# One explicit order for all TensorE instructions of a fused retention and adapter kernel

## The chip, the cores and the metric

The kernel runs on one core of a Trainium2 chip. The metric is the device time of one execution in microseconds, as the median of several runs. TensorE (PE) does the matrix work, VectorE (DVE), ScalarE (ACT) and GpSimd (POOL) the elementwise work, and SyncE (SP) issues nearly all transfers.

## The reference

Two steps follow each other. The first is a causal attention without softmax, in which the score of a query and a key is scaled by 1/8 and by a decay `gamma[h] ** (i - j)`; the second sends each token through two of eight adapters of rank 16.

```python
q, k, v: (8, 8, 576, 64) float32        # batch, heads, sequence, head dimension
scores = scale * q @ k.T
ret    = scores * where(i >= j, gamma[h] ** (i - j), 0)
x      = (ret @ v) as (4608, 512)       # 4608 tokens, 8 heads x 64
logits = x @ w_gate                     # (4608, 8)
w      = softmax over the two largest logits
out    = x + sum over those two e of  w_e * ((x @ A[e]) @ B[e])
```

All of `x @ A[e]` and `x @ w_gate` is made in one product with 128 + 8 columns; `z` is masked with the weights and goes through all of `B` in one product.

## The kernel before

The sequence of 576 is cut into four chunks of 128 rows and a last one of 64. A quad is four batch entries of one chunk: it is what one group of loads brings (twelve transfers of 256 KB, four each for q, k and v). A unit is two batch entries of one quad, all eight heads. There are 18 units: four per chunk for the four full chunks (units 0 to 15) and two for the short one (units 16 and 17). The sums over earlier chunks are carried in `P`, one per unit position, so unit t reads what unit t - 4 left.

For each unit t the program runs these stages, each a burst of TensorE instructions and the work of another engine on its result:

- T (L173, pqT and pkT, L186): 16 transposes of q and 16 of k, 64 rows by 128 columns each. `b` alternates fastest, so that neighbouring transposes take the lower and the upper 64 rows of the array. ACT copies the results to qT and kT (L195).
- Q (L201, px, L213): products of 64 by 64 with the carried sums, 32 instructions in the trace (a float32 product is two there, a transpose one); left out in the first chunk.
- S (L222, pe and pl, L238): the scores, 64 instructions in the trace; DVE multiplies them with the causal mask (re L250, rl L263).
- R (L269, px, L285): masked scores times v, on top of Q; DVE scales the result to xT (L297).
- U (L307, pu, L318): the new carried sum, 64 instructions; DVE adds the old one (pn L333) and POOL applies the decay (P L334).
- Z (L368, pz, L373): 16 instructions of the full 128 by 128 array; DVE then makes lg (L386), two maxima, ns (L389), cm (L399) and zc (L405), with a sigmoid on ACT between ns and cm.
- B, X and Y (L338, L356, L413) finish the unit: B transposes xT into po (16 instructions, L345), X transposes zc (pzt, L360), Y adds the product with `Bcat` to po (L421); ACT copies po to osb (L431), and SP stores it.

The main loop (L454 to L471) writes them in the order Q(t), S(t), T(t+1), B(t-1), R(t), U(t), X(t-1), Z(t), Y(t-1). POOL scales v for the next unit (L166). The loads of a quad are written two quads ahead, into three sets of buffers.

The order in the program text is not the order on the engines. A compile-time scheduler places the instructions of each engine by what it estimates to be ready, and the pools hand out buffers as it goes. Two pools lie in PSUM: `pxp` with two buffers for px, and `pp` with six buffers of one tag, which all other products share. A product that takes over a buffer waits until the engine that reads the earlier one is through. On the chip each engine then works through its own list in order.

Three shapes of array are used: 64 by 128 (the transposes T and B), 64 by 64 (Q, S, R, U) and 128 by 128 (X, Z, Y). In the order of the kernel before, the shape changes 165 times over 3036 products and transposes, and 318 transposes follow one that used the same 64 rows.

Of the kernel before, what the change touches and what calls it, by code (L numbers as in the profile page):

```python
# [18 lines left out]
def kernel(  # L19
# [10 lines left out]
    nc = tc.nc  # L30
# [34 lines left out]
    dr_first = nc.inline_tensor(id64_np, "c_first")  # L65
    dr_asc = nc.inline_tensor(asc_np.astype(np.float32), "c_asc")
    dr_rest = nc.inline_tensor(rest_np, "c_rest")

    cpool = ctx.enter_context(tc.tile_pool(name="consts", bufs=1))
    iop = ctx.enter_context(tc.tile_pool(name="io", bufs=3))  # L70
# [102 lines left out]
    def stage_T(t):  # L173
        c, qd, sl = units[t]
        full = c < NFULL
        qt, kt, vt = nat[(c, qd)]
        s = {}
        for nm in ("qT", "kT"):
            dst = wk.tile([128, 2, HP, C], FP32, tag=nm, name=nm)
            ps = [pp.tile([128, HP, 2, L], FP32, tag="pb", name=f"p{nm}") for _ in range(2)]  # L180
            for hp in range(HP):
                for x, (e, sx) in enumerate(parts(t)):
                    for b in range(2):
                        h2 = slice(2 * hp, 2 * hp + 2)
                        lhs = (kt if nm == "kT" else qt)[e][rows(b), sx, h2, :]
                        nc.tensor.matmul(  # L186
                            ps[b][:, hp, x, :],
                            lhsT=lhs,
                            rhs=id64[rows(b), :],
                            is_transpose=True,  # L190
                            start=True,
                            stop=True,
                        )
            for b in range(2):
                nc.scalar.copy(  # L195
                    out=dst[:, b].rearrange("p a (x i) -> p a x i", x=2), in_=ps[b]
                )
            s[nm] = dst
        st[t] = s

    def stage_Q(t):  # L201
        c, qd, sl = units[t]
        s = st[t]
        s["px"] = px = [pxp.tile([128, HP, C], FP32, tag="px", name="px") for _ in range(2)]
        if c == 0:
            return
        n = 1 if c < NFULL else 2
        w = C // n
        for hp in range(HP):
            for x in range(n):  # L210
                for ho in range(2):
                    for b in range(2):
                        nc.tensor.matmul(  # L213
                            px[b][rows(ho ^ b), hp, w * x : w * x + w],
                            lhsT=P[(qd, sl + x)][b][rows(ho), hp, :],
                            rhs=s["qT"][rows(ho), b, hp, w * x : w * x + w],
                            start=(hp == 0 and x == 0),
                            stop=False,
                            skip_group_check=True,
                        )  # L220

    def stage_S(t):  # L222
        c, qd, sl = units[t]
        full = c < NFULL
        s = st[t]
        pe = [pp.tile([128, HP, C], FP32, tag="pb", name=f"pe{ho}") for ho in range(2)]
        pl = [pp.tile([128, HP, L], FP32, tag="pb", name=f"pl{ho}") for ho in range(2)] if full else []
        for x in range(2):
            for hp in range(HP):
                for b in range(2):  # L230
                    for ho in range(2):
                        if x == 1 and full:
                            o = pl[ho][rows(b), hp, :]
                        else:
                            o = pe[ho][rows(b), hp, (L * x if not full else 0) : (C if full else L * x + L)]
                        i0 = L * x
                        i1 = C if full else L * x + L
                        nc.tensor.matmul(  # L238
                            o,
                            lhsT=s["kT"][rows(ho), b, hp, L * x : L * x + L],  # L240
                            rhs=s["qT"][rows(ho), b, hp, i0:i1],
                            start=(hp == 0 and (x == 0 or full)),
                            stop=True,
                            skip_group_check=True,
                        )
        s["re"], s["rl"] = [], []
        for ho in range(2):
            r = wk.tile([128, HP, C], FP32, tag=f"re{ho}", name=f"re{ho}")
            if full:
                nc.vector.tensor_tensor(  # L250
                    out=r, in0=pe[ho],
                    in1=triE.unsqueeze(1).broadcast_to((128, HP, C)), op=ALU.mult,
                )
            else:
                nc.vector.tensor_tensor(
                    out=r.rearrange("p a (x i) -> p (a x) i", x=2),
                    in0=pe[ho].rearrange("p a (x i) -> p (a x) i", x=2),
                    in1=tri.unsqueeze(1).broadcast_to((128, HP * 2, L)), op=ALU.mult,
                )
            s["re"].append(r)  # L260
        for ho in range(len(pl)):
            r = wk.tile([128, HP, L], FP32, tag=f"rl{ho}", name=f"rl{ho}")
            nc.vector.tensor_tensor(  # L263
                out=r, in0=pl[ho],
                in1=tri.unsqueeze(1).broadcast_to((128, HP, L)), op=ALU.mult,
            )
            s["rl"].append(r)

    def stage_R(t):  # L269
        c, qd, sl = units[t]  # L270
        full = c < NFULL
        s = st[t]
        px = s["px"]
        vt = nat[(c, qd)][2]
        for x, (e, sx) in enumerate(parts(t)):
            for hp in range(HP):
                for ho in range(2):
                    for b in range(2):
                        if full and x == 1:
                            w = s["rl"][ho][rows(b), hp, :]  # L280
                        elif full:
                            w = s["re"][ho][rows(b), hp, :]
                        else:
                            w = s["re"][ho][rows(b), hp, L * x : L * x + L]
                        nc.tensor.matmul(  # L285
                            px[b][rows(ho ^ b), hp, L * x : C if full else L * x + L],
                            lhsT=vt[e][rows(b), sx, 2 * hp + ho, :],
                            rhs=w,
                            start=(c == 0 and hp == 0 and x == 0),
                            stop=True,  # L290
                            skip_group_check=True,
                        )
        s["xT"] = []
        for b in range(2):
            xt = mo.tile([128, HP, C], FP32, tag="xT", name="xT", bufs=6)
            if full:
                nc.vector.tensor_tensor(out=xt, in0=px[b], in1=asc[b], op=ALU.mult)  # L297
            else:
                nc.vector.tensor_tensor(
                    out=xt.rearrange("p a (x i) -> p a x i", x=2),  # L300
                    in0=px[b].rearrange("p a (x i) -> p a x i", x=2),
                    in1=asc[b][:, :, 0:L].unsqueeze(2).broadcast_to((128, HP, 2, L)),
                    op=ALU.mult,
                )
            s["xT"].append(xt)

    def stage_U(t):  # L307
# [5 lines left out]
        for hp in range(HP):  # L313
            for e in range(2):
                for ho in range(2):
                    for b in range(2):
                        h = 2 * hp + ho
                        nc.tensor.matmul(  # L318
                            pu[b][rows(ho), hp, :],
                            lhsT=kt[e][rows(b), sl, h, :],  # L320
                            rhs=vt[e][rows(b), sl, h, :],
                            start=(hp == 0 and e == 0),
                            stop=(e == 1),
                            skip_group_check=True,
                        )
# [12 lines left out]
    def stage_B(t):  # L338
# [3 lines left out]
        for g in range(2):  # L342
            for dt in range(HP):
                for cc in range(2):
                    nc.tensor.matmul(  # L345
                        po[cc][:, g, dt, :],
                        lhsT=s["xT"][g][rows(cc), dt, :],
                        rhs=id64[rows(cc), :],
# [7 lines left out]
    def stage_X(t):  # L356
        s = st[t]
        pzt = pp.tile([128, 2, 128], FP16, tag="pb", name="pzt")
        for g in range(2):
            nc.tensor.matmul(  # L360
                pzt[:, g, :], lhsT=s["zc"][:, g, :], rhs=ident16,
                is_transpose=True, start=True, stop=True,
            )
# [4 lines left out]
    def stage_Z(t):  # L368
        s = st[t]
        pz = pp.tile([128, 2, ER + E], FP32, tag="pb", name="pz")  # L370
        for g in range(2):
            for dt in range(HP):
                nc.tensor.matmul(  # L373
                    pz[:, g, :],
                    lhsT=s["xT"][g][:, dt, :],
                    rhs=AW[g][:, dt, :],
# [36 lines left out]
    def stage_Y(t):  # L413
# [4 lines left out]
        bv = Bcat.rearrange("p (a o d) -> p a o d", a=HP, o=2)  # L418
        for cc in range(2):
            for g in range(2):  # L420
                nc.tensor.matmul(  # L421
                    po[cc][:, g, :, :],
                    lhsT=s["zT"][:, g, :],
                    rhs=bv[:, :, cc ^ g, :],
# [80 lines left out]
```

## Time and profile before

| | us |
|---|---|
| runs shown | 254.44, 257.71, 264.52 (median 257.71) |
| profiled execution | 254.11 |
| its span, first to last instruction | 251.9 |
| PE busy | 211.1 (84%) |
| DVE, ACT, POOL busy | 104.7, 76.7, 57.5 |
| mean granted clock | 0.968 |

A unit ends on TensorE with Z, and DVE starts lg within 0.1 us of that, so the starts of lg mark the units. A matmul of the trace is a pair with its weight load; matmuls overlap, so the length of a burst is read from the start of one burst to the start of the next. "x16" in a row is the number of instructions that were merged into it. The profile carries the line numbers of the kernel before.

### The profile page before, as it was taken

How to read it: one execution, taken by the hardware profiler on the slowest of the kernel's cores; microseconds unless marked ns; L12 is line 12 of the kernel's file. 1: busy time of each engine (PE TensorE's matmuls, PEld its weight loads, DVE VectorE, ACT ScalarE, POOL GpSimd, SP SyncE). 2: the span in 40 equal slices, each digit the busy share in tenths (PEclk: the TensorE clock that was granted, in tenths of full speed). 3: DMA queues.
4: the chain of work that ended last, by engine and by line, in shares of the span. 5: the costliest groups of instructions: out<-in, count | busy, mean ns of one | idle time of the engine just before them, and what ended most of it. 6: DMA issues, size and time to landing. Idle time of an engine off the chain costs nothing.

```text
span 251.9 us, 11229 instructions
## 1 busy us (share of the span) xinstructions
PE 211.1 (84%) x5100; PEld 183.3 (73%) x5100; DVE 104.7 (42%) x282; ACT 76.7 (30%) x200; POOL 57.5 (23%) x72
## 2 busy tenths in 40 slices
PE   1787989799998997989789879989798979997970
PEld 0576878687878785978678768878597868987850
DVE  0032262563235436551835254623555173474440
ACT  2302123521361123411243135313341124532431
POOL 1250204105002052203520080206220342071000
PEclk9996599999999999999999999999999999999995
DMA  5887798998998980689339940879178004831233
GB/s 114 215 130 163 175 226 201 222 229 207 203 274 193 222 222 4 173 197 204 103 108 202 225 145 18 218 175 233 37 191 227 9 0 138 196 113 69 85 87 83
DMA packets 123071, 39.29 MB, mean 156 GB/s; under 512 B 118032, under 2 KB 118288, under 8 KB 123024
## 3 DMA queue, kind: packets, MB, share of 16 engines
q1 hardware_dynamic: 122880, 38.44, 62.9%
q8 instruction: 40, 0.66, 1.1%
q0 software_dynamic: 144, 0.13, 0.3%
q14 instruction: 7, 0.06, 0.1%
HBM read 29.26 MB, written 9.44 MB: 154 GB/s over the span
## 4 chain that ended last, share of the span: by engine, by line
PE 63%; DVE 17%; SPq 7%; ACT 6%; issue 3%; DMA 1%; ACTq 0%; DVEq 0%
PE pz L373 15%; PE px L285 12%; PE px L213 8%; PE pu L318 7%; PE pkT L186 5%; PE pqT L186 5%; DVE cm L399 5%; SPq L126 5%; PE po L345 4%; DVE re L250 4%; PE pe L238 3%; ACT qT L195 3%; DVE ns L389 2%; DVE xT L297 2%; PE po L421 2%
## 5 line engine op out<-in xcount | busy, mean ns | idle before, releaser
L334 POOL TENSOR_TENSOR P<-pn,gdec 128x256 f32<-128x256 f32 x24 | 17.0, 729 | 126.1 <-DVE pn L333 126.1
L166 POOL TENSOR_TENSOR v<-v,pack 128x512 f32<-128x512 f32 x36 | 36.6, 1044 | 34.0 <-DMA v<-in_v_dram 34.0
L195 ACT COPY qT<-pqT 128x512 f32<-128x512 f32 x36 | 20.1, 588 | 69.3 <-PE pqT L186 69.3
L373 PE MATMUL pz<-AW,xT 128*128 128x136 f32 x288 | 40.0, 294 | 1.2 <-DVE pn L333 0.9
L297 DVE TENSOR_TENSOR xT<-px,asc 128x512 f32<-128x512 f32 x32 | 20.6, 686 | 43.8 <-PE px L285 43.8
L373 PEld LDWEIGHTS pz<-AW,xT 128*128 128x128 f32 x288 | 36.4, 198 | 2.2 <-ACT zT L365 1.1
L195 ACT COPY kT<-pkT 128x512 f32<-128x512 f32 x36 | 20.4, 595 | 55.6 <-PE pkT L186 55.5
L186 PE MATMUL pqT<-id,q 64*128 64x64 f32 x288 | 24.4, 238 | 7.6 <-DMA q<-in_q_dram 6.9
L285 PE MATMUL px<-re,v 64*64 64x128 f32 (+1 forms) x640 | 25.8, 272 | 4.1 <-issue 1.5
L186 PE MATMUL pkT<-id,k 64*128 64x64 f32 x288 | 27.0, 242 | 1.6 <-DMA k<-in_k_dram 1.1
L431 ACT COPY osb<-po 128x256 f32<-128x256 f32 x72 | 22.4, 395 | 16.4 <-PE po L421 16.4
L186 PEld LDWEIGHTS pqT<-id,q 64*128 64x128 f32 x288 | 18.8, 143 | 11.7 <-issue 6.8
L213 PE MATMUL px<-qT,P 64*64 64x128 f32 (+1 forms) x512 | 21.0, 264 | 5.0 <-DVE xT L297 4.2
L186 PEld LDWEIGHTS pkT<-id,k 64*128 64x128 f32 x288 | 20.0, 146 | 6.9 <-issue 2.5
L285 PEld LDWEIGHTS px<-re,v 64*64 64x64 f32 x640 | 18.5, 136 | 7.8 <-DVE re L250 3.2
L250 DVE TENSOR_TENSOR re<-pe,triE 128x512 f32<-128x512 f32 x32 | 20.5, 681 | 8.2 <-PE pe L238 8.1
L318 PE MATMUL pu<-v,k 64*64 64x64 f32 x1024 | 23.6, 227 | 0.2 <-ACT qT L195 0.2
L238 PE MATMUL pe<-qT,kT 64*64 64x128 f32 (+1 forms) x640 | 22.8, 271 | 0.9 <-ACT kT L195 0.9
L213 PEld LDWEIGHTS px<-qT,P 64*64 64x64 f32 x512 | 16.8, 133 | 7.7 <-ACT qT L195 4.0
L318 PEld LDWEIGHTS pu<-v,k 64*64 64x64 f32 x1024 | 20.3, 139 | 1.5 <-ACT qT L195 0.3
L238 PEld LDWEIGHTS pe<-qT,kT 64*64 64x64 f32 x640 | 18.7, 138 | 3.4 <-issue 1.7
L238 PE MATMUL pl<-qT,kT 64*64 64x64 f32 x512 | 14.2, 227 | 7.3 <-DVE zc L405 7.3
(35 smaller groups left out, 177.7 us busy)
## 6 DMA issues: line engine op xcount, KB each, us to landing
q<-in_q_dram SPq DMA_DIRECT2D x32, 256.0 KB, 5.1
k<-in_k_dram SPq DMA_DIRECT2D x32, 256.0 KB, 5.1
v<-in_v_dram SPq DMA_DIRECT2D x32, 256.0 KB, 5.1
out_dram<-osb SPq DMA_DIRECT2D x32, 256.0 KB, 3.3
q<-in_q_dram SPq DMA_DIRECT2D x8, 128.0 KB, 3.8
k<-in_k_dram SPq DMA_DIRECT2D x8, 128.0 KB, 3.4
v<-in_v_dram SPq DMA_DIRECT2D x8, 128.0 KB, 3.2
out_dram<-osb SPq DMA_DIRECT2D x8, 128.0 KB, 2.4
```

Source lines behind the costliest of these rows:

```text
L166: nc.gpsimd.tensor_tensor(out=vv, in0=vv, in1=gv[:, e].unsqueeze(2).broadcast_to((128, H, Dh)), op=ALU.mult,)
L186: nc.tensor.matmul(ps[b][:, hp, x, :], lhsT=lhs, rhs=id64[rows(b), :], is_transpose=True, start=True, stop=True,)
L195: nc.scalar.copy(out=dst[:, b].rearrange("p a (x i) -> p a x i", x=2), in_=ps[b])
L213: nc.tensor.matmul(px[b][rows(ho ^ b), hp, w * x : w * x + w], lhsT=P[(qd, sl + x)][b][rows(ho), hp, :], rhs=s["qT"][rows(ho), b, hp, w * ...
L238: nc.tensor.matmul(o, lhsT=s["kT"][rows(ho), b, hp, L * x : L * x + L], rhs=s["qT"][rows(ho), b, hp, i0:i1], start=(hp == 0 and (x == 0 or ...
L250: nc.vector.tensor_tensor(out=r, in0=pe[ho], in1=triE.unsqueeze(1).broadcast_to((128, HP, C)), op=ALU.mult,)
L285: nc.tensor.matmul(px[b][rows(ho ^ b), hp, L * x : C if full else L * x + L], lhsT=vt[e][rows(b), sx, 2 * hp + ho, :], rhs=w, start=(c == ...
L297: nc.vector.tensor_tensor(out=xt, in0=px[b], in1=asc[b], op=ALU.mult)
L318: nc.tensor.matmul(pu[b][rows(ho), hp, :], lhsT=kt[e][rows(b), sl, h, :], rhs=vt[e][rows(b), sl, h, :], start=(hp == 0 and e == 0), stop=( ...
L334: nc.gpsimd.tensor_tensor(out=pn, in0=tmp, in1=gdec, op=ALU.mult)
L373: nc.tensor.matmul(pz[:, g, :], lhsT=s["xT"][g][:, dt, :], rhs=AW[g][:, dt, :], start=(dt == 0), stop=(dt == HP - 1), skip_group_check=True,)
L431: nc.scalar.copy(out=osb[:, g, :, cc ^ g, :], in_=po[cc][:, g])
```

## The change

Every matmul and every transpose now goes through a helper `mm`, which gives it a dependency, without a semaphore, on the TensorE instruction that was written before it. So the scheduler must keep TensorE's instructions in the order of the program text. All nine calls of `nc.tensor.matmul` become `mm` with the same arguments; two of them are shown.

```diff
@@ -66,6 +66,17 @@
     dr_asc = nc.inline_tensor(asc_np.astype(np.float32), "c_asc")
     dr_rest = nc.inline_tensor(rest_np, "c_rest")
 
+    order = mybir.DependencyInfo(mybir.DependencyClass.NoSync, mybir.DependencyReason.DATA)
+    queued = {}
+
+    def mm(*args, **kw):
+
+        i = nc.tensor.matmul(*args, **kw)
+        i = getattr(i, "ins", i)
+        if "pe" in queued:
+            tc.add_manual_dep(i, queued["pe"].name, order, reason="program order")
+        queued["pe"] = i
+
...
@@ -183,7 +194,7 @@
                         lhs = (kt if nm == "kT" else qt)[e][rows(b), sx, h2, :]
-                        nc.tensor.matmul(
+                        mm(
                             ps[b][:, hp, x, :],
...
@@ -282,7 +293,7 @@
-                        nc.tensor.matmul(
+                        mm(
                             px[b][rows(ho ^ b), hp, L * x : C if full else L * x + L],
```

The counts over the new order are 74 changes of shape, and no transpose after one of the same 64 rows. The lists of DVE and SP keep their order; those of ACT and POOL change in places.

The first place is TensorE in unit 11, between S(11) and Z(11). Rows carry the line of the call, the operation, output and inputs with their buffer numbers, and the output's partitions by elements; pqT_2927 and pqT_2928 are the two halves of T(12), px_2864 and px_2865 belong to R(11). Before:

```order
L238 MATMUL pl1_2885<-qT_2683,kT_2704 64x64
L186 MATMUL pqT_2927<-id64_73,q320_2097 128x64
L186 MATMUL pqT_2928<-id64_73,q320_2097 128x64
L285 MATMUL px_2864<-re0_2918,v320_1597 64x128
L186 MATMUL pqT_2927<-id64_73,q321_2098 128x64
L186 MATMUL pqT_2927<-id64_73,q320_2097 128x64
L186 MATMUL pqT_2927<-id64_73,q321_2098 128x64
L186 MATMUL pqT_2927<-id64_73,q320_2097 128x64
L186 MATMUL pqT_2927<-id64_73,q321_2098 128x64
L186 MATMUL pqT_2927<-id64_73,q320_2097 128x64
L186 MATMUL pqT_2927<-id64_73,q321_2098 128x64
L285 MATMUL px_2865<-re0_2918,v320_1597 64x128
```

The same place now (L74 is the line inside the helper):

```order
L74 MATMUL pl1_2885<-qT_2683,kT_2704 64x64
L74 MATMUL pqT_2927<-id64_73,q320_2097 128x64
L74 MATMUL pqT_2928<-id64_73,q320_2097 128x64
L74 MATMUL pqT_2927<-id64_73,q321_2098 128x64
L74 MATMUL pqT_2928<-id64_73,q321_2098 128x64
L74 MATMUL pqT_2927<-id64_73,q320_2097 128x64
L74 MATMUL pqT_2928<-id64_73,q320_2097 128x64
L74 MATMUL pqT_2927<-id64_73,q321_2098 128x64
L74 MATMUL pqT_2928<-id64_73,q321_2098 128x64
```

R(11) stood between the transposes and split them by halves; now the 32 transposes of T(12) and the 16 of B(10) stand together ahead of R(11), and the halves alternate.

The second place is TensorE around the end of Z(11): pz_3069 is Z(11), pkT_2949 one half of T(12), po0_2968 and po1_2969 are Y(10), px_3116 and px_3117 are Q(12), pe0_3134 is S(12). Before:

```order
L373 MATMUL pz_3069<-AW1_82,xT_3020 128x136 x4
L186 MATMUL pkT_2949<-id64_73,k321_2100 128x64
L186 MATMUL pkT_2949<-id64_73,k320_2099 128x64
L186 MATMUL pkT_2949<-id64_73,k321_2100 128x64
L186 MATMUL pkT_2949<-id64_73,k320_2099 128x64
L186 MATMUL pkT_2949<-id64_73,k321_2100 128x64
L186 MATMUL pkT_2949<-id64_73,k320_2099 128x64
L186 MATMUL pkT_2949<-id64_73,k321_2100 128x64
L421 LDWEIGHTS zT_3067
L421 MATMUL po0_2968<-Bcat_83,zT_3067 128x256
```

Now:

```order
L74 MATMUL pz_3069<-AW1_82,xT_3020 128x136 x4
L74 LDWEIGHTS zT_3067
L74 MATMUL po0_2968<-Bcat_83,zT_3067 128x256
L74 LDWEIGHTS zT_3067
L74 MATMUL po0_2968<-Bcat_83,zT_3067 128x256
L74 LDWEIGHTS zT_3067
L74 MATMUL po1_2969<-Bcat_83,zT_3067 128x256
L74 LDWEIGHTS zT_3067
L74 MATMUL po1_2969<-Bcat_83,zT_3067 128x256
L74 MATMUL px_3116<-qT_2926,P000_2309 64x128
L74 MATMUL px_3117<-qT_2926,P001_2313 64x128
```

The late half of the k transposes is gone from here, and Q(12), which stood before U(11), has moved behind Y(10).

The third place is POOL in units 8 and 9: P_2309 and P_2313 belong to unit 8, P_2552 and P_2556 to unit 9, and v_1597 and v_1598 are the v of the quad of units 10 and 11. Before:

```order
L334 TENSOR_TENSOR P_2309<-pn_2310,gdec 128x256
L334 TENSOR_TENSOR P_2313<-pn_2314,gdec 128x256
L334 TENSOR_TENSOR P_2552<-pn_2553,gdec 128x256
L334 TENSOR_TENSOR P_2556<-pn_2557,gdec 128x256
L166 TENSOR_TENSOR v_1597<-v_1597,pack 128x512 x2
L166 TENSOR_TENSOR v_1598<-v_1598,pack 128x512 x2
```

Now:

```order
L345 TENSOR_TENSOR P_2309<-pn_2310,gdec 128x256
L345 TENSOR_TENSOR P_2313<-pn_2314,gdec 128x256
L177 TENSOR_TENSOR v_1597<-v_1597,pack 128x512 x2
L345 TENSOR_TENSOR P_2552<-pn_2553,gdec 128x256
L345 TENSOR_TENSOR P_2556<-pn_2557,gdec 128x256
L177 TENSOR_TENSOR v_1598<-v_1598,pack 128x512 x2
```

The four scalings of v that followed every second unit are now two after each unit.

## Rows read from the trace of the kernel before

**Rows 1.** The page: span, busy time by engine, the main DMA queue.

```profile
span 251.9 us, 11229 instructions
...
PE 211.1 (84%) x5100; PEld 183.3 (73%) x5100; DVE 104.7 (42%) x282; ACT 76.7 (30%) x200; POOL 57.5 (23%) x72
...
q1 hardware_dynamic: 122880, 38.44, 62.9%
```

**Rows 2.** Windows: stretch, length, busy PE PEld DVE ACT POOL, clock, DMA share, GB/s.

```profile
24.00:31.00 7.00, 7.00 (x54) 6.15 (x58) 0.87 (x3) 1.17 (x2) 2.08 (x2) 0.50 0.76 171
67.40:223.50 156.10, 138.39 (x3505) 121.19 (x3506) 72.86 (x192) 50.26 (x133) 37.01 (x45) 1.00 0.62 156
```

**Rows 3.** DVE timeline, lg after Z(1), Z(3), Z(15), Z(17): start, length, instruction.

```profile
42.15 0.17 DVE L386 COPY lg<-pz 128x16 f32<-128x16 f32 x1 [1.88 <-PE pz L373]
...
67.41 0.17 DVE L386 COPY lg<-pz 128x16 f32<-128x16 f32 x1 [1.88 <-PE pz L373]
...
223.56 0.17 DVE L386 COPY lg<-pz 128x16 f32<-128x16 f32 x1 [1.24 <-PE pz L373]
...
242.79 0.17 DVE L386 COPY lg<-pz 128x16 f32<-128x16 f32 x1 [1.61 <-PE pz L373]
```

**Rows 4.** PE timeline in units 10 and 11; in brackets idle time and releaser.

```profile
151.46 0.69 PE L238 MATMUL pl<-qT,kT 64*64 64x64 f32 x30 [1.46 <-DVE zc L405]
...
155.19 1.10 PE L285 MATMUL px<-re,v 64*64 64x128 f32 x32
...
157.63 0.28 PE L360 MATMUL pzt<-ident,zc 128*128 128x128 f16 x2
157.77 2.09 PE L373 MATMUL pz<-AW,xT 128*128 128x136 f32 x16
...
165.31 0.64 PE L186 MATMUL pqT<-id,q 64*128 64x64 f32 x7
...
167.11 1.47 PE L213 MATMUL px<-qT,P 64*64 64x128 f32 x26 [0.89 <-DVE xT L297]
...
169.09 0.76 PE L345 MATMUL po<-id,xT 64*128 64x64 f32 x16
169.78 1.14 PE L318 MATMUL pu<-v,k 64*64 64x64 f32 x58
```

**Rows 5.** PE timeline of unit 15, S and the q transposes in one piece.

```profile
215.64 0.64 PE L238 MATMUL pl<-qT,kT 64*64 64x64 f32 x32
216.21 0.71 PE L186 MATMUL pqT<-id,q 64*128 64x64 f32 x16
216.76 0.65 PE L186 MATMUL pkT<-id,k 64*128 64x64 f32 x8
```

**Rows 6.** DVE timeline after Z(9) and after Z(10).

```profile
147.70 0.17 DVE L386 COPY lg<-pz 128x16 f32<-128x16 f32 x1 [1.88 <-PE pz L373]
...
149.37 1.64 DVE L399 SCALAR_TENSOR_TENSOR cm<-lg,m,sg 128x8 f32<-128x8 f32 x2 [0.37 <-ACT sg L394]
150.93 0.48 DVE L405 TENSOR_TENSOR zc<-pz,cm 128x128 f16<-128x128 f32 x2
...
159.90 0.17 DVE L386 COPY lg<-pz 128x16 f32<-128x16 f32 x1 [1.01 <-PE pz L373]
...
161.37 0.48 DVE L405 TENSOR_TENSOR zc<-pz,cm 128x128 f16<-128x128 f32 x2
162.26 1.29 DVE L250 TENSOR_TENSOR re<-pe,triE 128x512 f32<-128x512 f32 x2 [0.41 <-PE pe L238]
163.46 0.74 DVE L263 TENSOR_TENSOR rl<-pl,pack 128x256 f32<-128x256 f32 x2
```

**Rows 7.** POOL timeline after Z(9).

```profile
146.94 4.05 POOL L166 TENSOR_TENSOR v<-v,pack 128x512 f32<-128x512 f32 x4
```

**Rows 8.** SP timeline: issues of quad 1's k; the page's DMA issues: median landing.

```profile
28.86 4.64 SPq L126 DMA_DIRECT2D k<-in_k_dram  x4
...
k<-in_k_dram SPq DMA_DIRECT2D x32, 256.0 KB, 5.1
```

**Rows 9.** PE timeline in Z(0): twelve of its sixteen instructions.

```profile
27.76 3.09 PE L373 MATMUL pz<-AW,xT 128*128 128x136 f32 x12
```

More of the change, by code (lines that the diff above doesn't have):

```diff
@@ L237, in stage_S @@
                         i1 = C if full else L * x + L
-                        nc.tensor.matmul(
+                        mm(
                             o,
@@ L284, in stage_R @@
                             w = s["re"][ho][rows(b), hp, L * x : L * x + L]
-                        nc.tensor.matmul(
+                        mm(
                             px[b][rows(ho ^ b), hp, L * x : C if full else L * x + L],
@@ L317, in stage_U @@
                         h = 2 * hp + ho
-                        nc.tensor.matmul(
+                        mm(
                             pu[b][rows(ho), hp, :],
@@ L344, in stage_B @@
                 for cc in range(2):
-                    nc.tensor.matmul(
+                    mm(
                         po[cc][:, g, dt, :],
@@ L359, in stage_X @@
         for g in range(2):
-            nc.tensor.matmul(
+            mm(
                 pzt[:, g, :], lhsT=s["zc"][:, g, :], rhs=ident16,
@@ L372, in stage_Z @@
             for dt in range(HP):
-                nc.tensor.matmul(
+                mm(
                     pz[:, g, :],
@@ L420, in stage_Y @@
             for g in range(2):
-                nc.tensor.matmul(
+                mm(
                     po[cc][:, g, :, :],
```

## The prediction

> **What bounds the kernel now.** I read the page first: TensorE is busy 84% of the span, DVE 42%, and the main DMA queue 62.9% [rows 1]. So TensorE or the waits around it set the time. The windows come next. From 67.4 to 223.5 us, over units 4 to 15, the granted clock is 1.00 and TensorE is busy 138.39 of 156.10 us [rows 2]. The starts of lg give the pace: Z(3) ends at 67.41 and Z(15) at 223.56, so twelve units take 156.15 us, 13.0 each [rows 3].
>
> The TensorE timeline then shows what these 13.0 us hold [rows 4]. Three things are to be seen. Seven q transposes of one half take 0.64 us; sixteen that alternate between the halves take 0.71 us [rows 5]. So a late half costs almost as much as a whole stage. Q(12) waits 0.89 us for xT and pl waits 1.46 us for zc. And R and U, 64 instructions each, take 2.44 us where they stand undisturbed (155.19 to 157.63), Z takes 2.13 us to the lg behind it (157.77 to 159.90 in [rows 6]).
>
> The last view is DVE after Z [rows 6]. From lg to the end of zc it needs 1.95 us in unit 11 (159.90 to 161.85) and 3.71 us in unit 10 (147.70 to 151.41). In the slow case POOL is scaling v for 4.05 us at the same time [rows 7], and cm takes 1.64 us.
>
> **The change, part by part.** It removes and adds no work. It moves TensorE's instructions back into the program's order, and POOL's scaling of v in pairs behind each unit. I therefore build one unit of the new order from steps of the old trace, beginning at lg.
>
> - DVE: lg to zc. With four scalings of v in the way the chain is 3.71 us, with none 1.95. Now two of them, half the 4.05 us, follow each unit's P and so meet each chain. I take the middle of the two rows, 2.83, rounded to 2.9; both ends stay for the range.
> - DVE: re and rl, 162.26 to 164.20, 1.94 us. re could not begin before 2.36 after lg in unit 11, since S's pe ended then; at 2.9 it follows zc. So rl ends at 2.9 + 1.94 = 4.84.
> - TensorE beside it: pl can wait for zc, as it did for 1.46 us, because a pl may take over pz's buffer. From 2.9 on it needs pl 0.57 and pqT 0.55 [rows 5], and pkT like pqT, 0.55: 4.57. The transposes wait in part for re's buffers, since pqT or pkT may take over pe's. All this fits under the DVE leg, so T costs nothing; if DVE were faster, T would be the leg from 4.57 less what it gains.
> - B takes over pl's buffers, so it starts when rl is through: 0.05 for the hand-over and 0.69 (169.09 to 169.78) [rows 4].
> - R and U 2.44, X 0.14 (157.63 to 157.77), Z 2.13. xT and pn are made beside U. zT is made beside Z, and osb beside the next Q and S.
>
> The sum is 4.84 + 0.05 + 0.69 + 2.44 + 0.14 + 2.13 = 10.29 us a unit. With zc unblocked, re starts at 2.36 and the unit is 9.75; with the whole 3.71 it is 11.1. Twelve units at 10.29 are 123.5 us, **32.7 us less** than 156.15.
>
> The Trainium skill, SBUF — State Buffer, section "Who interferes with whom", says that a DVE instruction with two SBUF inputs and a GpSimd instruction that reads SBUF exclude each other, the loser waiting for the winner's whole instruction. ns and cm have two such inputs, and the stretched rows agree. By that rule each of them would wait for what is left of one scaling, about 0.65 us in sum instead of 0.95, and the twelve units would be some 3.6 us shorter.
>
> **The start.** TensorE must now take T(2) before B(0) and R(1), whatever has arrived. The last of quad 1's k is issued before 33.50 and lands 5.1 us after its issue [rows 8], at about 38. Behind it stand pkT 0.55, B 0.69, R and U 2.44, X 0.14 and Z 2.13: Z(1) ends at 44.0 instead of 42.15 [rows 3], 1.8 later. The wait of some 4 us may also bring the clock down. From 24 to 31 us it was 0.50 with TensorE wholly busy [rows 2], and twelve instructions of Z took 3.09 us instead of 1.57 [rows 9]. Wholly at half clock these 5.95 us would cost 5.9 more, at full clock nothing. I take 1.2, since such a stretch need not last through all of them. So Z(1) ends at 45.15. Units 2 and 3, which have no Q, I take at 9.8, by the same legs: Z(3) at 64.75, **2.7 us earlier** than 67.41.
>
> **The end.** Units 16 and 17 took 19.2 us [rows 3]. Without U, half of the 2.44, a unit is 9.1; the last one has no T either and its R no long wait, 8.2. That is 17.3, **1.9 us less** (bounds 0 and 3). The 9.1 us behind Z(17) are serial already and stay.
>
> Span: 251.9 - 32.7 - 2.7 - 1.9 = 214.6. The profiled execution was 254.11, 2.2 more than its span, so **217 us**. It lay below the median of the runs shown, 257.71, by 3.6 us; I keep these for the upper end.
>
> **The loads** do not bind: over units 4 to 15 the DMA engines were busy 0.62 of 156.1 us, 96.8 us of work; in 123.5 us that is 0.78. A quad's data is written two quads ahead, and its wait shows only at the start.
>
> **The rivals.**
>
> 1. *The waits come back (chance 0.20).* A list in order cannot fill a wait. Unit 10 had most of its stages in the program's order already and still took 12.20 us (147.70 to 159.90). If each unit ends there, twelve take 146.4, 9.8 less; with nothing won at the start that is 244 us, and between 235 and 246. For it: pl's wait of 1.46 us stands in just that unit [rows 4]. Against it: 1.76 of its 12.20 us is the doubled stretch of the zc chain (3.71 against 1.95), which the two scalings per unit should halve.
> 2. *Slower: the clock falls (0.05).* TensorE now has one wait in each unit at the same place, and 48 transposes in one piece. One unit's TensorE steps add up to about 2.2 (lg to pl, a little less than the 2.36 to re) + 0.57 + 1.10 + 0.69 + 2.44 + 0.14 + 2.13 = 9.2 us. At half clock, by the 3.09 against 1.57, that is near 18: twelve units would take 66 us longer than now, about 320 us. It decides as soon as the mean clock over these units is under 0.76, where 9.2 / 0.76 + 0.9 reaches 13.0. Against it: in unit 10 nothing but transposes stands between pl, which ends at 152.15, and R at 155.19 [rows 4], 3 us, and the clock of the whole stretch was 1.00 [rows 2]. The Trainium skill, TensorE: Matmul & The Clock Gate, "Part 4: PE-mode transpose", says that transposes do not count as activity in the same way and leave the clock at its lower level; by it this rival would be likely, but the row just named speaks against it.
> 3. *Nothing is gained (0.05).* Either the order does not change what is waited for, or transfers set the pace: a pair of units would need 26 us for its loads and stores, where their share of 0.62 leaves 16.1. That the order stays is excluded by the lists, in which 318 transposes of the same half become none. About 254 us.
>
> **Numbers and chances.** The forecast of 217 has 0.70. Its own ends are 207 (unit 9.75, which is 6.5 less, no loss of clock at the start, 1.2 less, and 1 to 2 less at the end) and 231 (unit 11.1, 9.7 more, and the whole 4.7 of the half clock at the start). With the 3.6 us between the profiled execution and the median the upper end is 235, where the first rival begins. Runs of this kernel spread by some 4%, so 2% is about what can be told from no change. Faster than that holds for the forecast and the first rival, 0.90; within it 0.05; slower 0.05.
>
> **What would show it.** The lg rows should stand about 10.3 us apart in units 4 to 15. Every T should be two rows of sixteen, 0.7 us each, and no row of seven. pl should wait for zc, or pkT or B for re or rl, by 0.5 to 1 us in each unit. ns or cm should be stretched in nearly every unit instead of every second. T(2) should wait for k until about 38 us. The clock should be 1.00 from 50 us on. The forecast is wrong if the pace stays near 12 us with new waits ahead of R, or if the clock or the transfers fall behind.

## The result and the profile after

| | before | after |
|---|---|---|
| median of the runs, us | 256.85 (254.44 to 264.52) | 225.08 (221.98 to 228.06) |
| profiled execution, its span, us | 254.11, 251.9 | 228.06, 226.0 |
| PE busy over units 4 to 15 | 138.39 of 156.10 us | 117.02 of 131.93 us |

The ratio is 0.872, with an interval of 0.859 to 0.886; it is formed, like those below, of the fast runs of both kernels, those within 1.5% of the fastest. The profiled execution was the longest of its four, so spans and rows below stand some 3 us above the median.

The page answers to [rows 1]: span, busy time, granted clock in 40 slices, main DMA queue, and the queue that carries instructions.

```profile
span 226.0 us, 11231 instructions
...
PE 181.0 (80%) x5100; PEld 163.1 (72%) x5100; DVE 100.0 (44%) x282; ACT 74.7 (33%) x200; POOL 57.5 (25%) x72
...
PEclk9999996799999999999999999999999999999995
...
q1 hardware_dynamic: 122880, 38.44, 70.0%
q8 instruction: 40, 0.66, 1.2%
```

TensorE worked 30 us less for the same 5100 instructions, and the data queue filled more of the shorter span. The window over units 4 to 15 answers to [rows 2]; its columns are the same.

```profile
66.75:198.68 131.93, 117.02 (x3530) 107.43 (x3529) 69.48 (x193) 48.47 (x132) 39.18 (x47) 1.00 0.74 186
```

The DVE timeline of after: lg after Z(1), Z(3), Z(4), Z(5), Z(6), Z(12), Z(13), Z(15), Z(17) [rows 3], behind Z(6) the chain that answers to [rows 6], and behind Z(12) its rows cm and re.

```profile
45.98 0.17 DVE L397 COPY lg<-pz 128x16 f32<-128x16 f32 x1 [1.09 <-PE pz L74]
...
66.75 0.17 DVE L397 COPY lg<-pz 128x16 f32<-128x16 f32 x1 [1.37 <-PE pz L74]
...
76.98 0.17 DVE L397 COPY lg<-pz 128x16 f32<-128x16 f32 x1 [1.10 <-PE pz L74]
...
90.08 0.17 DVE L397 COPY lg<-pz 128x16 f32<-128x16 f32 x1 [1.37 <-PE pz L74]
...
100.53 0.17 DVE L397 COPY lg<-pz 128x16 f32<-128x16 f32 x1 [1.30 <-PE pz L74]
...
101.01 0.41 DVE L400 SCALAR_TENSOR_TENSOR ns<-m 128x2 f32<-128x2 f32 x1
101.79 0.78 DVE L410 SCALAR_TENSOR_TENSOR cm<-lg,m,sg 128x8 f32<-128x8 f32 x2 [0.37 <-ACT sg L405]
102.49 0.48 DVE L416 TENSOR_TENSOR zc<-pz,cm 128x128 f16<-128x128 f32 x2
102.90 1.29 DVE L261 TENSOR_TENSOR re<-pe,triE 128x512 f32<-128x512 f32 x2
...
168.45 0.17 DVE L397 COPY lg<-pz 128x16 f32<-128x16 f32 x1 [1.32 <-PE pz L74]
...
169.68 0.77 DVE L410 SCALAR_TENSOR_TENSOR cm<-lg,m,sg 128x8 f32<-128x8 f32 x2 [0.37 <-ACT sg L405]
...
170.81 1.29 DVE L261 TENSOR_TENSOR re<-pe,triE 128x512 f32<-128x512 f32 x2
...
178.12 0.17 DVE L397 COPY lg<-pz 128x16 f32<-128x16 f32 x1 [1.09 <-PE pz L74]
...
198.68 0.17 DVE L397 COPY lg<-pz 128x16 f32<-128x16 f32 x1 [1.37 <-PE pz L74]
...
216.67 0.17 DVE L397 COPY lg<-pz 128x16 f32<-128x16 f32 x1 [1.61 <-PE pz L74]
```

Unit 4 takes 10.23 us and unit 6 takes 10.45, but unit 5 takes 13.10. Unit 13 (168.45 to 178.12) is the shortest with 9.67. Units 4 to 15 take 131.93 us. TensorE's timeline shows the kinds: T(2) at the start, the middle of unit 4, and the long gaps of units 5 and 8.

```profile
36.40 0.36 PE L74 MATMUL pkT<-id,k 64*128 64x64 f32 x1 [1.39 <-DMA k<-in_k_dram]
38.36 1.00 PE L74 MATMUL pkT<-id,k 64*128 64x64 f32 x13 [1.60 <-DMA k<-in_k_dram]
...
69.58 0.71 PE L74 MATMUL pqT<-id,q 64*128 64x64 f32 x16
70.12 0.22 PE L74 MATMUL pkT<-id,k 64*128 64x64 f32 x1
70.56 0.70 PE L74 MATMUL pkT<-id,k 64*128 64x64 f32 x15 [0.21 <-DVE re L261]
71.04 0.88 PE L74 MATMUL po<-id,xT 64*128 64x64 f32 x16
71.85 1.10 PE L74 MATMUL px<-re,v 64*64 64x128 f32 x32
...
74.87 2.07 PE L74 MATMUL pz<-AW,xT 128*128 128x136 f32 x16
...
87.57 0.34 PE L74 MATMUL pu<-v,k 64*64 64x64 f32 x8 [2.05 <-issue]
...
122.17 0.28 PE L74 MATMUL pzt<-ident,zc 128*128 128x128 f16 x2 [2.25 <-issue]
```

Unit 4 has the order that was forecast: T whole, a short wait of pkT for re, then B, R, U, Z, with one gap of 0.20 us in R. The gap at 87.57 stands in the middle of U, between two products of one burst, and "issue" says that nothing in the profile releases it. The list of TensorE's waits over units 4 to 15 of after (sum in us, times, longest) shows that such waits are most of what is left:

```profile
PE pu L74 <- issue: 5.0, 5, 2.1
PE pzt L74 <- issue: 2.3, 1, 2.3
PE px L74 <- issue: 2.3, 4, 1.0
PE pz L74 <- issue: 1.8, 1, 1.8
PE pkT L74 <- DVE re L261: 1.6, 7, 0.3
PE pl L74 <- DVE zc L416: 0.9, 3, 0.4
PE po L74 <- issue: 0.6, 1, 0.6
```

They are 12.0 us. The same list of before, over its units 4 to 15, was another one:

```profile
PE pl L238 <- DVE zc L405: 7.3, 5, 1.5
PE px L213 <- DVE xT L297: 3.9, 5, 0.9
...
PE px L213 <- issue: 0.6, 1, 0.6
```

**What the gaps are.** I numbered all entries of TensorE in the trace of after (matmuls, weight loads, and the 88 entries of its sequencer between them), and set beside the gaps the packets of the queue "instruction" (40 packets, each of 16,384 bytes):

```
place in TensorE's list      3265    4290    5058    5569    6849
remainder by 256              193     194     194     193     193
16-KB packet landed, us     86.35  106.33  120.86  131.19  155.02
TensorE goes on, us         87.57  107.81  122.17  132.75  156.32
waited, us                   2.05    1.04    2.25    1.41    1.78
```

All 14 such gaps over 0.3 us behind 40 us have the remainder 193 or 194. So TensorE's own list comes by DMA, 256 entries of 64 bytes at a time, and where a block lands late TensorE stands still until 1.2 to 1.6 us after its landing. The Trainium skill, Runtime: NRT & Kernel Launch, "Instruction fetch mechanics", gives the same block, 16 KiB or 256 instructions, and calls the cost of crossing one mostly hidden; here it was not: the 14 gaps are 13.9 us in a span of 226.0.

### The profile page after: what moved, and what is told of

It reads as the page before. It is cut to its first block, busy times and chain, and to the rows that moved or that the text cites. A ratio compares the mean times of both kernels' runs of the same rounds, so it can differ in the third digit from the quotient of the medians.

```text
span 226.0 us, 11231 instructions
## 1 busy us (share of the span) xinstructions
PE 181.0 (80%) x5100; PEld 163.1 (72%) x5100; DVE 100.0 (44%) x282; ACT 74.7 (33%) x200; POOL 57.5 (25%) x72
## 4 chain that ended last, share of the span: by engine, by line
PE 57%; DVE 14%; SPq 13%; issue 8%; DMA 3%; ACT 2%; ACTq 0%
PE px L74 16%; PE pz L74 15%; SPq L137 11%; PE pu L74 7%; PE po L74 7%; DVE re L261 5%; PE pkT L74 4%; PE pe L74 4%; DVE cm L410 3%; DMA k<-in_k_dram 3%; DVE ns L400 2%; PE pzt L74 2%; DVE zc L416 2%; SPq L109 1%; PE pqT L74 1%
## 5 line engine op out<-in xcount | busy, mean ns | idle before, releaser
L74 PE MATMUL pz<-AW,xT 128*128 128x136 f32 x288 | 37.9, 283 | 3.0 <-issue 1.8
L74 PEld LDWEIGHTS pz<-AW,xT 128*128 128x128 f32 x288 | 34.8, 190 | 3.7 <-issue 2.1
L74 PE MATMUL pu<-v,k 64*64 64x64 f32 x1024 | 20.6, 225 | 6.4 <-issue 6.4
L74 PE MATMUL pkT<-id,k 64*128 64x64 f32 x288 | 18.6, 243 | 8.7 <-DMA k<-in_k_dram 5.3
L74 PE MATMUL pqT<-id,q 64*128 64x64 f32 x288 | 16.1, 240 | 11.5 <-DMA q<-in_q_dram 10.3
L74 PE MATMUL px<-re,v 64*64 64x128 f32 (+1 forms) x640 | 22.7, 280 | 1.9 <-issue 1.7
L376 ACT COPY zT<-pzt 128x256 f16<-128x256 f16 x18 | 6.7, 372 | 52.8 <-PE pzt L74 52.8
L74 PEld LDWEIGHTS pu<-v,k 64*64 64x64 f32 x1024 | 18.4, 140 | 7.3 <-issue 7.3
L74 PEld LDWEIGHTS pqT<-id,q 64*128 64x128 f32 x288 | 12.4, 146 | 14.1 <-issue 9.9
L74 PEld LDWEIGHTS pkT<-id,k 64*128 64x128 f32 x288 | 13.9, 149 | 11.6 <-DMA k<-in_k_dram 4.9
L74 PE MATMUL pe<-qT,kT 64*64 64x128 f32 (+1 forms) x640 | 21.3, 268 | 0.7 <-ACT kT L206 0.6
L74 PEld LDWEIGHTS px<-re,v 64*64 64x64 f32 x640 | 18.0, 141 | 3.6 <-issue 1.9
L74 PEld LDWEIGHTS pe<-qT,kT 64*64 64x64 f32 x640 | 18.1, 137 | 1.7 <-ACT kT L206 1.0
L74 PE MATMUL po<-id,xT 64*128 64x64 f32 x288 | 15.5, 233 | 0.8 <-issue 0.6
L74 PE MATMUL px<-qT,P 64*64 64x128 f32 (+1 forms) x512 | 16.1, 262 | 0.0
```

The source lines that it names most:

```text
L74: i = nc.tensor.matmul(*args, **kw)
L376: nc.scalar.copy(out=zt, in_=pzt)
```

## The experiments

Each kernel was timed beside runs of the kernel before on the same chip. The medians of the kernel before lie between 256.32 and 259.95 us from chip to chip, so ratios are compared where they are given; where none is, the range of the runs stands instead.

**The change again.** The same code, to have it on the same chip as the next runs.

> The change itself once more, beside the other three. 225 us, within 221 to 229; units without a TensorE wait for nothing in the profile about 10.3 us apart at lg, and some 14 us of such waits in all.

Measured: 221.21 us, ratio 0.859 (0.830 to 0.887). Its waits without a releaser were 9.4 us in a span of 220.4. Against 14.6 in 226.0, counted alike, that is 5.2 of the 5.6 us by which the two profiles differ: between these two, late blocks are most of the scatter. Its units 4, 7 and 13, which hold no late block, take 9.67 or 9.68 us, not the 10.3 that was expected.

**Few loads.** Quads 3 and later take the buffers of the first three instead of loading theirs.

```diff
+        if n >= 3:
+            nat[(c, qd)] = nat[quads[n - 3]]
+            return
```

> The change, but only the first three quads are loaded; the later ones read the same buffers again, so seven tenths of the input traffic are left out. Theory (blocks of TensorE's own instruction list are fetched late where the data transfers fill the DMA engines): the waits before TensorE for which the profile names nothing fall from 14 us to under 3, and units 5, 8, 9 and 11 take about 10.3 us like the rest: 210 to 216 us. Rival (TensorE uses its list up faster than it can be fetched, whatever else moves): the same waits, 222 to 226 us.

Measured: 209.97 us, ratio 0.825 (0.809 to 0.840). Waits without a releaser fell to 2.0 us, and ten of the twelve units became equal; two of its lg rows:

```profile
133.51 0.17 DVE L400 COPY lg<-pz 128x16 f32<-128x16 f32 x1 [1.09 <-PE pz L74]
143.19 0.17 DVE L400 COPY lg<-pz 128x16 f32<-128x16 f32 x1 [1.09 <-PE pz L74]
```

They take 9.66 to 9.68 us each; the other two, each with a late block, take 10.33 and 10.23. The list has as many blocks as ever (40), so it is the data transfers that hold them up. The packets show where: behind 50 us, a block's packet begins on average 2.08 us after TensorE enters the block before it in the change, and 0.77 us after with few loads, while the packet itself takes 1.10 us in both. That TensorE merely uses its list up too fast, the rival, is excluded: here it went through a block in 4.24 us on average, in the change in 4.72. One side effect: without waiting for v, POOL scales earlier, and ns and cm take 0.16 and 0.41 in most units. It is not where the gain comes from, since in unit 4 they take 0.40 and 0.78 and the unit takes 9.67 all the same.

**No lock.** ns becomes a negated sum, and cm reads the logits from PSUM, so neither has two inputs in SBUF.

```diff
-        nc.vector.scalar_tensor_tensor(
-            out=ns, in0=m8[:, :, 0], scalar=-1.0, in1=m8[:, :, 1],
-            op0=ALU.mult, op1=ALU.subtract,
+        nc.vector.tensor_reduce(
+            out=ns, in_=m8[:, :, 0:2], op=ALU.add, axis=mybir.AxisListType.X, negate=True,
...
-                out=cm[:, g, :], in0=lg[:, g, :], ...
+                out=cm[:, g, :], in0=pz[:, g, ER : ER + E], ...
```

> The change, with cm reading the logits from PSUM and ns made by a reduction, so that neither has two inputs in SBUF while GpSimd scales v. Theory (the chain from lg over zc and rl leads each unit, and GpSimd stretches it): ns 0.2 us, cm 0.2 us each, zc through 2.0 us after lg, undisturbed units 9.75 instead of 10.3 us; 218 to 222 us. Rival (TensorE's own list sets the pace): 224 to 226 us, with longer waits for nothing that the profile names.

Measured: 220.00 us, ratio 0.850 (0.828 to 0.871). On DVE, while POOL scaled v from 131.63 to 133.67:

```profile
132.28 0.16 DVE L400 TENSOR_REDUCE ns<-m 128x2 f32<-128x4 f32 x1
132.81 0.42 DVE L409 SCALAR_TENSOR_TENSOR cm<-pz,m,sg 128x8 f32<-128x8 f32 x2 [0.37 <-ACT sg L404]
```

So the stretch is gone beside a scaling, and that unit takes 9.67 us. It is what the prediction drew from the Trainium skill (SBUF — State Buffer, "Who interferes with whom"), now shown by taking the second SBUF input away. Yet the time is that of the change, for two reasons. The stretch delays little: unit 13 of the change takes 9.67 too, with cm at 0.77, and re begins 2.36 us after lg there as here; only where ns and cm are stretched most (0.60 and 0.77, in units 8, 11 and 14) does zc put re off, to 2.55. And 12.5 us went into late blocks here, where the change again had 9.4.

**T chained alone.** The kernel before, with only the 32 transposes of each T kept in order.

```diff
+        queued.clear()
         for nm in ("qT", "kT"):
...
-                        nc.tensor.matmul(ps[b][:, hp, x, :], ...
+                        mm(ps[b][:, hp, x, :], ...
```

> The kernel before, with only the 32 transposes of each T chained among themselves: no transpose follows one of the same half any more, but the stages stay mixed, with 171 changes of array shape. Theory (what cost was the change of shape and the waits, not the halves): 252 to 259 us, like before. Rival (the late halves cost by themselves, 318 times 28 ns): 244 to 249 us.

Measured: 263.21 us, ratio 1.011 (1.003 to 1.019). The halves alternate again everywhere, with 171 changes of shape, and nothing is won: the rival falls. By the ratio the theory, like before, holds to 1%; the 252 to 259 us that I gave for it were too low.

**Halves apart.** The change, with `b` as the outermost loop of T.

```diff
-            for hp in range(HP):
-                for x, (e, sx) in enumerate(parts(t)):
-                    for b in range(2):
+            for b in range(2):
+                for hp in range(HP):
+                    for x, (e, sx) in enumerate(parts(t)):
```

> The change, but with the loops of T turned round, so that all transposes of the lower half come before those of the upper half; the order of the stages stays. Theory (a transpose behind one of the same half costs twice; T lies beside the DVE leg only as long as it takes 1.1 us): T takes 2.3 to 2.5 us, each unit 1.0 to 1.4 us more, 238 to 246 us. Rival (the gain comes from the fewer changes of array shape and from the stages' order alone): 224 to 228 us.

Measured: 220.13 us, ratio 0.864 (0.850 to 0.879), below both forecasts, and a clear miss for the theory. T and B together take 2.31 us (65.67 to 67.98), where their own work in the alternating order is 1.8 to 1.9. But in unit 4 of the change the same stretch takes 2.27 (69.58 to 71.85) with its waits for re: the slower transposes fill time that is waited away otherwise, and unit 4 here takes 9.67 us.

**B in U.** The change, with the 16 transposes of B(t-1) in four pieces, each behind a quarter of U(t): 179 changes of shape.

```diff
+            if t > 0:
+                piece_B(t - 1, hp)
```

> The change, but with the sixteen transposes of B(t-1) cut into four pieces that stand between the quarters of U(t): 179 changes of array shape instead of 74, no work more, and R no longer behind B. Theory (a change of shape costs TensorE about 0.2 us): some 105 changes more are 21 us, 236 to 246 us. Rival (the changes cost nothing, the gain came from waits that went away): 215 to 225 us.

Measured: 228.22 us (224.06 to 231.05), between the two forecasts. One unit, first and last rows of U and its pieces:

```profile
73.26 0.41 PE L74 MATMUL pu<-v,k 64*64 64x64 f32 x16
73.61 0.34 PE L74 MATMUL po<-id,xT 64*128 64x64 f32 x4
...
75.86 0.28 PE L74 MATMUL pzt<-ident,zc 128*128 128x128 f16 x2
```

U and B take 2.60 us in place of 1.05 + 0.7 or 0.8. That is some 0.8 for seven more changes, 0.11 each, half of what I had expected. By that the 91 changes that the change removes are some 10 us, an estimate. The Trainium skill, TensorEngine Tiling (Array Packing), "Key Properties", says that a change of mode drains the array; it gives no price, and these rows give an estimate of one.

**Wide transposes.** Each pair of 64-row transposes in T and B becomes one of 128 rows, and the copies are rearranged to fit.

```diff
-                    for b in range(2):
-                        lhs = (kt if nm == "kT" else qt)[e][rows(b), sx, h2, :]
-                        mm(ps[b][:, hp, x, :], lhsT=lhs, rhs=id64[rows(b), :], ...
+                    lhs = (kt if nm == "kT" else qt)[e][:, sx, h2, :]
+                    mm(ps[hp // 2][:, 2 * (hp % 2) + x, :], lhsT=lhs, rhs=id64, ...
```

> The change, with each pair of 64-row transposes in T and B made as one of 128 rows: 432 instructions and as many weight loads fewer, so a tenth less of TensorE's list to fetch, and T and B take the array shape of X, Z and Y. Theory (the fetch of the list is the wait that is left): waits for nothing named fall from 10 to 14 us to under 9, 212 to 219 us. Rival (the number of instructions is not what holds it): 219 to 226 us.

Measured: 218.72 us, ratio 0.834 (0.826 to 0.843), as the theory had it. Waits without a releaser are 1.3 us. Eight wide transposes take 0.9 us (67.12 to 68.05) where sixteen narrow ones took 0.55, so T is longer and the units take 10.1 to 10.9, one 11.5.

**Wide transposes and no lock.** Both edits together.

> The wide transposes and, as in the run without the two SBUF inputs, ns and cm free of GpSimd. Theory: a unit of 9.7 us where nothing is fetched late and fewer late fetches, 207 to 215 us. Rival (the loads set the pace of the list): like the wide transposes alone, within 1%.

Measured: 215.12 us (213.92 to 217.12), ratio 0.828 (0.820 to 0.836), the lowest of the kernels that load all their data, and just above what was expected. But its ratio lies within 1% of that of the wide transposes alone, as the rival had it, so the times do not show a gain of the one over the other. The pace does: eight of the twelve units take 10.1 to 10.2 us.

```profile
167.18 0.17 DVE L397 COPY lg<-pz 128x16 f32<-128x16 f32 x1 [1.10 <-PE pz L74]
177.32 0.17 DVE L397 COPY lg<-pz 128x16 f32<-128x16 f32 x1 [1.10 <-PE pz L74]
```

That is 0.5 above the 9.67 of narrow transposes, but with 1.9 us of late blocks instead of the 12.5 of no lock alone. Which of the two did it, 37 blocks instead of 40 or entries that each take longer, was not separated.

**Q early.** The change, with Q(t+1) between R(t) and U(t).

```diff
+        if t + 1 < NU:
+            stage_Q(t + 1)
         stage_U(t)
```

> The change, but Q(t+1) is written between R(t) and U(t), where the scheduler of the kernel before had put it; the number of changes of array shape stays the same as in the change. Theory (the place of Q is the gain): in the change Q runs behind Z and Y while DVE works on zc, where TensorE has nothing else that is ready, and costs nothing. Between R and U it lies on the path with its own 1.2 us and, since px has two buffers, waits for xT, which took 0.89 us in the kernel before. That is 2.1 us a unit, 14 units 29 us, less about 3 for the shorter way to S: 244 to 250 us, against 221 for the change, and a wait px <- DVE xT of 0.8 to 1 us in nearly every unit. Rival (the gain lies in the bursts that are no longer broken, the place of Q does not matter since TensorE has the same work): 219 to 226 us.

Measured: 248.71 us (242.57 to 250.66), as the theory had it. On TensorE in unit 9, between R and U:

```profile
138.04 0.64 PE L74 MATMUL px<-rl,v 64*64 64x64 f32 x32
139.57 0.40 PE L74 MATMUL px<-qT,P 64*64 64x128 f32 x2 [0.89 <-DVE xT L308]
140.17 0.99 PE L74 MATMUL px<-qT,P 64*64 64x128 f32 x27 [0.20 <-DVE xT L308]
```

With the same bursts and the same changes of shape most of the gain is gone: a unit is 12.2 us (lg at 132.13 and 144.36). The place of Q decides, because behind Z it fills time in which TensorE has nothing else, while between R and U it is paid in full and waits for xT. My text for this run said that the kernel before had it there; that holds for odd units alone ([rows 4], Q(12) in unit 11).

**Late half of k.** The change, with the second half of the k transposes of T(t+1) behind Z(t); q's transposes also stand half by half.

```diff
+        if t + 1 < NU:
+            st[t + 1]["late"](1)
         if t > 0:
             stage_Y(t - 1)
```

> The change, but the transposes of the second half of k for unit t+1 stand behind Z(t) and ahead of Y(t-1), where the scheduler of the kernel before had often put them; 33 more changes of shape, and the halves of k no longer alternate. Theory (a late half costs by what waits for it): S(t+1) waits for it and for the copy on ACT, so pe ends near lg + 3.0 instead of lg + 2.3, later than zc at 2.4 to 2.6, and the unit gets 0.4 to 0.7 longer: 226 to 232 us against 221. Rival (a short burst of one half and the two changes of shape cost by themselves, about 0.6 us a unit, and what waits for it adds to that): 233 to 240 us. If the zc chain hides all of it: 219 to 224 us.

Measured: 227.06 us, ratio 0.886 (0.878 to 0.894), as the theory had it, though the interval overlaps with those of the change. The rows are clearer: pe ends 3.05 us after lg where it ends 2.31 after lg in unit 13 of the change, and the units without a late block take 10.1 to 10.9 us.

**Both edits.** Q early and the late half of k together.

> The change with both edits of this call: Q(t+1) between R(t) and U(t), and the second half of k behind Z(t). Theory (the place of Q is most of the gain): the late half fills the time that Q has left behind Z and is hidden by zc, so the time is that of Q early alone, 244 to 250 us, plus 0 to 4. Rival (the two add up, each being a part of what the mixed order cost): 252 to 262 us, the time of the kernel before.

Measured: 243.90 us, ratio 0.953 (0.943 to 0.962): not more than Q early alone. The two do not add up; the late half takes the place that Q left behind Z.

**Pairs.** Q early in odd units only, and v scaled by fours behind each odd unit, as in the kernel before.

```diff
+        if t % 2 and t < 15:
+            stage_Q(t + 1)
         stage_U(t)
+        if t % 2 and t < 15:
+            scale_v(t + 1)
+            scale_v(t + 2)
```

> The change with two things placed as the scheduler of the kernel before had them, and nothing else: Q(t+1) between R(t) and U(t) in odd units t only, and POOL's scaling of v as four in one go behind each odd unit's P instead of two behind each unit (POOL's multiplications chained in that order too). Bursts stay whole, 74 changes of shape as in the change. In the kernel before, odd units such as unit 11 take 14.62 us and even ones such as unit 10 take 12.20. Theory (these two placements are about a third of the gain, the rest lies in the broken and mixed bursts of T, R and Q): an even unit has no Q, but zc ends 3.7 after lg, so 3.7 + 1.94 + 0.05 + 0.69 + 2.44 + 0.14 + 2.13 = 11.1 us; an odd one has no scaling beside zc, 9.7 us, and 2.1 for Q and its wait for xT, 11.8 us. A pair is 22.9 us against 20.6 to 20.9 for the change without late blocks of the list: seven pairs give 14 to 16 us, 233 to 241 us in all. Rival (the two placements are the whole gain, the mixed bursts cost nothing): pairs of 26 to 27 us and 250 to 258 us.

Measured: 239.96 us (236.84 to 241.58), within the 233 to 241 of the theory. Three of its lg rows, after Z(11), Z(12) and Z(13), and a window inside unit 12, with its columns as in [rows 2]:

```profile
164.50 0.17 DVE L404 COPY lg<-pz 128x16 f32<-128x16 f32 x1 [1.31 <-PE pz L74]
176.34 0.17 DVE L404 COPY lg<-pz 128x16 f32<-128x16 f32 x1 [1.14 <-PE pz L74]
188.59 0.17 DVE L404 COPY lg<-pz 128x16 f32<-128x16 f32 x1 [1.28 <-PE pz L74]
...
168.80:172.00 3.20, 3.20 (x64) 3.08 (x64) 0.83 (x3) 2.05 (x4) 0.00 (x0) 0.50 0.95 225
```

An even unit takes 11.84 us, an odd one 12.25, a pair 24.1. In the kernel before the pair of units 10 and 11 takes 26.8 (12.20 and 14.62), in the change the seven units of 4 to 15 without a gap over 0.6 us take 9.67 to 10.54, 10.24 on average, so a pair takes 20.5. Of the 6.3 us that a pair wins, 3.6 come from the places of Q and of the scalings, and 2.7 from the rest of the order, above all from bursts that are whole. The rival, that the two places are all of it, is ruled out. But the 3.6 hold a loss of clock that neither the kernel before nor the first profile of the change has (both 1.00 over units 4 to 15): in unit 12, behind a wait of pl for zc of 1.89 us, the granted clock was 0.50 for a stretch, T and B took 2.67 us and R and U 2.91. In unit 6, at 1.00, T and B took 1.78, and R and U at 1.00 take 2.43. That is some 1.4 us, an estimate; without it the two places would be 2.2 of the 6.3 and the rest 4.1, near the third that the theory gave. So the split lies between these two readings.

## Why the prediction was right, and where it was short

**The unit** was forecast at 10.29 us and is 10.24 on average in the seven units without a long gap. That agreement is luck, since two errors cancel. The first is the leg from lg over zc to R. Its first term, 2.9 for zc, took the middle of two rows; measured, re begins 2.36 us after lg in seven of the twelve units, when pe is through, and 2.71 at most, though ns and cm are stretched in 9 of the 12, by 0.5 to 0.8 us in sum, less than the 0.95 of the forecast. In unit 13 re begins at 2.36 and R at 5.00 (forecast 5.58), R and U take 2.43 (2.44), X 0.12 (0.14) and Z with the lg behind it 2.11 (2.13): 9.67 us, near the 9.75 that the prediction had as its lower end. The second is that the other six of the seven units are longer, mostly by short late blocks: in unit 4 one of 0.20 us in R makes R and U 2.90. In unit 13 TensorE's only wait is 0.23 us for re, so the legs of TensorE and of DVE are nearly even there. The wait of 0.5 to 1 us for zc, re or rl, which was to show in each unit, is 0.2 to 0.4 where it shows.

**"The loads do not bind"** is the step that failed. TensorE waits for no q, k or v after the start, and the share of the DMA engines, 0.74, is near the forecast 0.78. But the same engines carry the list, and its late blocks are 12.0 us of waits over units 4 to 15. The twelve units took 131.93 us where 123.5 were forecast, 8.4 more: 15.9 above twelve units of 9.67, most of it in the late blocks and in the 0.2 to 0.3 us that most of them cost beyond their gap, less the 7.4 by which these are shorter than the forecast ones. Few loads showed it from the one side, the wide transposes from the other.

**The start.** T(2) waited for k until 38.36 us, forecast about 38. The clock did fall beside this wait: from 36.0 to 42.5 us it was 0.50. From 38.36 to the end of Z(1) went 7.62 us, 1.67 above the 5.95 of full clock, where the forecast put 1.2. Z(1) ended at 45.98 (forecast 45.15), Z(3) at 66.75 (64.75), 2.0 late: 0.8 were lost by Z(1), late blocks at 53.14 and 63.54 us took 1.5, and units 2 and 3 were otherwise 0.3 shorter than forecast. **The end** took 17.99 us instead of 17.3, with 0.81 for a block in R(17). Behind Z(17) were 9.3 us.

In sum the span is 11.4 us over the forecast 214.6: 2.0 at the start, 8.4 in units 4 to 15, 0.7 and 0.2 at the end. The profiled execution lay 3 above the median, so the median is 8 above 217.

**The reasons.** That a late half costs almost as much as a whole stage was true of the row, and I took the halves, and in the texts of the runs the changes of shape, for the cause. The runs say otherwise: T chained alone wins nothing, halves apart cost nothing in a whole order, and a change of shape is some 0.1 us, an estimate. What I used without naming it was that the sum puts Q behind Z, under the zc chain. **The rivals:** waits came back in the form of late blocks, not of pl or Q as I had drawn it, and cost 8.4 of the 22.9 us that it would have taken over these units. The clock stayed at 1.00, its higher level, through units 4 to 15, with 48 transposes in one piece; the Trainium skill's rule on transposes (TensorE: Matmul & The Clock Gate, "Part 4: PE-mode transpose") does not show here, though with transposes some 1.9 us of a unit this is a weak test of it.

**Open.** How the 2.7 to 4.1 us a pair that the two places do not explain divide between halves that nothing hides, changes of shape and the late half of k in the mixed order was not tried apart. That the loads delay the packets of the list is shown; what on the way of a packet they delay is not.

## What to carry to other kernels

Read from the trace which stage an engine can run while another works on the critical result, and put that stage there by hand; an order made from estimates put Q where it was paid twice, once in full and once as a wait. When waits named "issue" appear in the middle of a burst, number the engine's list, with all its entries: if they stand 256 entries apart, the list itself comes late. Here fewer transfers took most of these waits away, and so did fewer and longer instructions. A stretched instruction costs only what it puts off: here ns and cm were stretched in most units, and re began hardly later for it. And where two errors of a forecast cancel, only the parts show it, so compare each term with its row, in a unit that nothing disturbs.

## What the runs showed of the hardware

A late block can also cost clock, and need not. In the first profile of the change waits of 2.05 and 2.25 us left the granted clock at 1.00. In the change again TensorE stood still for 1.98 us until 115.64, and right behind that the clock was 0.50, while Z, with the lg behind it, took 3.30 us instead of 2.11 (columns as in [rows 2]):

```profile
116.60:119.80 3.20, 3.20 (x15) 2.60 (x14) 0.57 (x4) 0.31 (x2) 1.28 (x2) 0.50 1.02 231
```

In the Q-early kernel TensorE waited 0.88 us for xT and, inside the next U, 2.35 for a block; the granted clock of that stretch fell below 1.00, and Z took 3.48 us from its start to Y (79.37 to 82.85) instead of 1.9. The window, with its columns as in [rows 2]:

```profile
74.00:83.10 9.10, 6.42 (x116) 5.83 (x117) 1.43 (x4) 0.37 (x1) 3.45 (x4) 0.81 0.94 236
```

Its mean of 0.81 lies between the two levels of 1.2 and 2.4 GHz: part of the stretch ran at the lower one. Transposes of 64 rows follow each other in 34 ns when the halves alternate (0.54 us for sixteen in unit 4), while eight of 128 rows took 0.93 us, 116 ns each.
